# A 2:4-sparse linear layer: one of four rows of the mask product on GpSimd

## The chip, the cores and the metric

The kernel runs on one core of one Trainium2 chip. The metric is the device time of one execution in microseconds (us), the median of several runs. The engines of the core are named as the profile names them: PE (TensorE, matrix products; PEld is its weight loading), DVE (VectorE), ACT (ScalarE), POOL (GpSimd) and SP (SyncE, which here only issues DMAs). Each engine works through its own queue of instructions in order; semaphores order them against each other.

## The reference

```python
B, S, D = 16, 512, 1024          # x: [B,S,D], w: [D,D], b: [D], all bfloat16
def reference(x, w, b):
    N, M = 2, 4
    G = D // M
    wg = w.reshape(G, M, D)
    mag = jnp.abs(wg)
    order = jnp.argsort(mag, 1)
    thr = jnp.take_along_axis(mag, order[:, M - N:M - N + 1, :], 1)
    mask = (lambda x, dt: x.astype(dt))(mag >= thr, w.dtype)
    wp = (wg * mask).reshape(D, D)
    return jnp.einsum("bsd,df->bsf", x, wp) + b
```

Of every four rows of the weight that follow each other, each column keeps the two largest magnitudes and zeroes the others; then comes a dense product of 8192 tokens with the 1024 x 1024 weight, and the bias.

## The kernel before

**Layout of the weight.** The weight is loaded with the four rows of a group side by side in one partition: a tile is [128 partitions, 4, columns], and the index 0 to 3 is the row m of the group. The largest and smallest of pairs, and so the threshold, are then plain elementwise operations along the free dimension.

**Pieces.** The masking is cut into eight pieces (g, first column, last column), g being the half of the input dimension: pieces 0 and 1 are 128 columns each, pieces 2 to 6 are 256, piece 7 is 512. For each, `abs_piece` takes magnitudes (on ACT for pieces 1 and 3 to 7, on DVE for 0 and 2), and `prep_piece` runs seven DVE instructions: hi and lo (largest and smallest of the pairs, L127 and L128), t1 and t2 (L131, L132), the threshold thr (L134), the mask (L136) and the product of the weight with the mask (L137). With 256 columns, mask and product are instructions over 128 x 1024 elements; with 512 columns over 128 x 2048. The mask tile comes from a pool of two buffers, so a mask two pieces later writes into the same memory.

**The front phase.** Seven token tiles (T = 7, 128 tokens each) are multiplied while the weight is still being masked. The order of all engines' work is written out by hand in the string `FRONT` and is kept: W is a dummy matmul, A an abs, P a `prep_piece`, Tgt the transposition of token tile t's half g on PE (four transposes, then a copy to SBUF on ACT, L154), and Mit the four matmuls of piece i for token tile t, one for each row m = 0 to 3 (`mm_piece`, L161). M20 is thus piece 2 for token tile 0, and its fourth matmul, m = 3, reads row 3 of the piece. V copies the finished left half of a bank to SBUF on ACT (L176), S adds the bias to it on DVE (L180), U (`unpack`) starts four DMAs that bring the masked weight into natural order, `wp_nat`, for the main phase (L144, on SP's queue), and B starts a transposing DMA of a batch of token tiles (L197, on SP's queue too).

After the string come the matmuls of piece 7, M70 to M76, with 512 columns, each token tile followed by DVE's addition of the bias out of the bank (`evac_dve`, L184) and a store from ACT's queue (L188).

**The main phase.** Token tiles 7 to 63 are multiplied from `wp_nat` and the transposed batches, 16 matmuls of 512 columns per tile (`mm_nat` at L248 for the first batch and the last tile, L286 for the rest), over eight PSUM banks in turn.

GpSimd builds the identity matrix for the transposes at the start (L101) and has nothing else to do.

Of the kernel before, what the change touches and what calls it, by code (L numbers as in the profile page):

```python
# [10 lines left out]
def kernel(  # L11
# [7 lines left out]
    nc = tc.nc  # L19
# [4 lines left out]
    Alu = mybir.AluOpType  # L24
    Act = mybir.ActivationFunctionType
    K = tc.keep_in_program_order
# [30 lines left out]
    def w_of(i):  # L57
        g, c0, c1 = pieces[i]
        for k, (lg, l0, l1) in loads.items():
            if lg == g and l0 <= c0 and c1 <= l1:  # L60
                return w_ld[k][:, :, c0 - l0:c1 - l0]

    def wp_of(i):
        g, c0, c1 = pieces[i]
        return wp_gh[(g, c0 // FH)][:, :, c0 % FH:c0 % FH + c1 - c0]
# [54 lines left out]
    def prep_piece(i):  # L120
        g, c0, c1 = pieces[i]
        n = c1 - c0
        mag = mags.pop(i)
        magv = mag.rearrange("p (a j) f -> p a j f", j=2)
        hi = tmp.tile([P, 2, FH], bf16, name="hi")[:, :, :n]
        lo = tmp.tile([P, 2, FH], bf16, name="lo")[:, :, :n]
        K(nc.vector.tensor_tensor(hi, magv[:, :, 0, :], magv[:, :, 1, :], op=Alu.max))  # L127
        K(nc.vector.tensor_tensor(lo, magv[:, :, 0, :], magv[:, :, 1, :], op=Alu.min))  # L128
        t1 = tmp.tile([P, FH], bf16, name="t1")[:, :n]
        t2 = tmp.tile([P, FH], bf16, name="t2")[:, :n]  # L130
        K(nc.vector.tensor_tensor(t1, hi[:, 0, :], hi[:, 1, :], op=Alu.min))  # L131
        K(nc.vector.tensor_tensor(t2, lo[:, 0, :], lo[:, 1, :], op=Alu.max))  # L132
        thr = tmp.tile([P, FH], bf16, name="thr")[:, :n]
        K(nc.vector.tensor_tensor(thr, t1, t2, op=Alu.max))  # L134
        mask = tmp.tile([P, 4, FH], bf16, name="mask")[:, :, :n]
        K(nc.vector.tensor_tensor(mask, mag, thr[:, None, :].to_broadcast([P, 4, n]), op=Alu.is_ge))  # L136
        K(nc.vector.tensor_tensor(wp_of(i), w_of(i), mask, op=Alu.mult))  # L137

    wp_nat = [const.tile([P, KT, FH], bf16, name=f"wp_nat{h}") for h in range(2)]

# [74 lines left out]
    for tok in FRONT.split():  # L215
        k, n = tok[0], [int(c) for c in tok[1:]]
        if k == "W":
            warm(1)
        elif k == "A":
            abs_piece(n[0], n[0] in ABS_ON_ACT)  # L220
        elif k == "P":
            prep_piece(n[0])
        elif k == "T":
            g, t = n
            transpose_half(g, t, t if g == 0 else T)
        elif k == "M":
            i, t = n
            mm_piece(i, t, start=i in (0, 5), stop=i in (4, 7))
        elif k == "V":
            evac_act(n[0])  # L230
        elif k == "S":
            add_staged(n[0], 0)
        elif k == "U":
            unpack(*n)
        elif k == "B":
            issue_batch(*batches[n[0]])
# [84 lines left out]
```

## Time and profile before

| | us |
|---|---|
| median of 3 runs (235.44 to 235.93) | 235.66 |
| the profiled execution | 236.1 |
| its span (first to last instruction) | 234.3 |
| PE busy in it | 228.1 |
| DVE busy | 105.7 |
| ACT busy | 18.5 |
| POOL busy | 0.7 |
| product with the mask (L137), 128x512, 128x1024, 128x2048 | 0.426, 0.692, 1.224 |

The span is the time between the first and the last profiled instruction; the execution's time has 1.8 us more around it. A timeline line reads: start in us from the span's start, length, engine, line, operation, output<-inputs, shapes, count; in brackets the engine's idle time before it and what ended it. A line of the groups reads: line, engine, operation, names, shapes, count | busy us, mean ns of one | idle time before and its releaser. The granted TensorE clock was 1.0 for the profiled execution.

### The profile page before, as it was taken

The page shows a single profiled execution, that of the slowest core. Times are in us where ns is not written, and L with a number is a line of the kernel's source. Part 1 is how long each engine was busy: PE and PEld are TensorE (multiplying, and loading weights), DVE is VectorE, ACT ScalarE, POOL GpSimd, SP SyncE. Part 2 cuts the span into 40 slices and gives each one's busy share as a digit, 9 for nine tenths or more (in the row PEclk, how much of TensorE's full clock was granted, in tenths as well). Part 3 has the DMA queues.
Part 4 walks back from the last instruction along what each step waited for, and adds up shares of the span by engine and source line. Part 5 has one row for each costly group of instructions (what it writes and reads, how often), then busy time and mean ns, then how long its engine had stood idle before and what let it go on. Part 6 is the DMA issues. An engine that isn't in the chain of part 4 may idle for free.

```text
span 234.3 us, 2922 instructions
## 1 busy us (share of the span) xinstructions
PE 228.1 (97%) x1197; PEld 114.6 (49%) x1216; DVE 105.7 (45%) x189; ACT 18.5 (8%) x29; POOL 0.7 (0%) x6
## 2 busy tenths in 40 slices
PE   6999999999999999999999999999999999999994
PEld 2889844444444444444444444444444444444453
DVE  3999995342442343344244234334324424433433
ACT  3899000000000000000000000000000000000000
POOL 1000000000000000000000000000000000000000
DMA  6999799999822399216952289221996221122122
GB/s 174 352 243 236 170 210 187 279 209 349 239 93 92 93 213 276 90 48 160 286 151 77 90 215 278 90 92 55 260 304 195 85 90 73 61 90 92 45 90 90
DMA packets 75292, 38.19 MB, mean 163 GB/s; under 512 B 60176, under 2 KB 67088, under 8 KB 75280
## 3 DMA queue, kind: packets, MB, share of 16 engines
q1 hardware_dynamic: 65392, 20.84, 42.6%
q10 hardware_dynamic: 9888, 17.17, 20.3%
q8 instruction: 9, 0.15, 0.3%
q14 instruction: 3, 0.02, 0.0%
HBM read 4.19 MB, written 16.78 MB: 90 GB/s over the span
## 4 chain that ended last, share of the span: by engine, by line
PE 93%; DMA 3%; DVE 2%; issue 1%; SPq 0%
PE bank L286 75%; PE bank L161 9%; PE bank L248 9%; DMA w_B<-in_w_dram 3%; PE bank L152 1%; DVE mask L136 0%; DVE wp L137 0%; SPq L76 0%; SPq L69 0%; DVE mag L116 0%; DVE o_sb L264 0%; DVE hi L127 0%; DVE lo L128 0%; DVE thr L134 0%; DVE t L132 0%
## 5 line engine op out<-in xcount | busy, mean ns | idle before, releaser
L286 PE MATMUL bank<-wp_nat,xTb 128*128 128x512 bf16 x753 | 165.1, 379 | 0.8
L184 DVE TENSOR_TENSOR o_sb<-bank,bias_sb 128x512 bf16<-128x512 f32 x119 | 76.7, 686 | 119.9 <-PE bank L286 108.6
L286 PEld LDWEIGHTS <-xTb 128*128 128x128 bf16 x768 | 75.1, 98 | 90.6
L161 PE MATMUL bank<-wp,xT 128*128 128x256 bf16 (+2 forms) x223 | 26.6, 272 | 0.4
L161 PEld LDWEIGHTS <-xT 128*128 128x128 bf16 x224 | 19.5, 98 | 5.6 <-ACT xT L154 0.7
L248 PE MATMUL bank<-wp_nat,xTs 128*128 128x512 bf16 (+1 forms) x110 | 21.0, 348 | 0.1
L248 PEld LDWEIGHTS <-xTs 128*128 128x128 bf16 x112 | 11.0, 98 | 10.0
L286 PE MATMUL bank<-wp_nat,xTs 128*128 128x512 bf16 x47 | 10.5, 379 | 0.1
L154 ACT COPY xT<-bank 128x512 bf16<-128x512 bf16 x14 | 7.7, 589 | 1.8 <-PE bank L152 1.8
L286 PEld LDWEIGHTS <-xTs 128*128 128x128 bf16 x48 | 4.7, 97 | 5.7
L136 DVE TENSOR_TENSOR mask<-mag,thr 128x1024 bf16<-128x1024 bf16 (+2 forms) x8 | 5.5, 692 | 0.3
L152 PE MATMUL bank<-ident,xh 128*128 128x128 bf16 x56 | 4.8, 219 | 0.7 <-DMA xh<-in_x_dram 0.6
L152 PEld LDWEIGHTS <-xh 128*128 128x128 bf16 x56 | 3.9, 114 | 1.8 <-DMA xh<-in_x_dram 1.5
L105 PE MATMUL bank<-zeros 128*128 128x512 bf16 x8 | 3.5, 625 | 1.2 <-DVE zeros L97 1.2
L180 DVE TENSOR_TENSOR o_sb<-stage,bias_sb 128x512 bf16<-128x512 f32 x7 | 4.3, 682 | 0.0
L176 ACT COPY stage<-bank 128x512 f32<-128x512 f32 x7 | 3.8, 627 | 0.3 <-PE bank L161 0.3
L127 DVE TENSOR_TENSOR hi<-mag 128x512 bf16<-128x512 bf16 (+2 forms) x8 | 3.4, 420 | 0.4 <-ACT mag L114 0.3
L128 DVE TENSOR_TENSOR lo<-mag 128x512 bf16<-128x512 bf16 (+2 forms) x8 | 3.3, 417 | 0.0
L134 DVE TENSOR_TENSOR thr<-t,t 128x256 bf16<-128x256 bf16 (+2 forms) x8 | 2.3, 292 | 0.3
L105 PEld LDWEIGHTS <-zeros 128*128 128x128 bf16 x8 | 1.0, 140 | 2.8 <-issue 1.7
L131 DVE TENSOR_TENSOR t<-hi 128x256 bf16<-128x256 bf16 (+2 forms) x8 | 2.3, 284 | 0.0
L132 DVE TENSOR_TENSOR t<-lo 128x256 bf16<-128x256 bf16 (+2 forms) x8 | 2.3, 284 | 0.0
(21 smaller groups left out, 17.4 us busy)
## 6 DMA issues: line engine op xcount, KB each, us to landing
out_dram<-o_sb ACTq DMA_DIRECT2D x63, 256.0 KB, 3.4
wp_nat<-wp SPq DMA_DIRECT2D x16, 128.0 KB, 2.7
xh<-in_x_dram SPq DMA_DIRECT2D x3, 256.0 KB, 6.1
xh<-in_x_dram ACTq DMA_DIRECT2D x2, 256.0 KB, 5.2
w_C<-in_w_dram SPq DMA_DIRECT2D x1, 512.0 KB, 6.9
w_D<-in_w_dram SPq DMA_DIRECT2D x1, 512.0 KB, 7.9
w_E<-in_w_dram SPq DMA_DIRECT2D x1, 512.0 KB, 8.9
xh<-in_x_dram SPq DMA_DIRECT2D x1, 384.0 KB, 6.8
```

Of the source, the lines that this page charges most:

```text
L105: K(nc.tensor.matmul(bank[7][:], lhsT=zeros[:, :P], rhs=zeros[:], start=True, stop=True))
L127: K(nc.vector.tensor_tensor(hi, magv[:, :, 0, :], magv[:, :, 1, :], op=Alu.max))
L128: K(nc.vector.tensor_tensor(lo, magv[:, :, 0, :], magv[:, :, 1, :], op=Alu.min))
L136: K(nc.vector.tensor_tensor(mask, mag, thr[:, None, :].to_broadcast([P, 4, n]), op=Alu.is_ge))
L152: K(nc.tensor.transpose(dst[:, m, :], xv[:, m, :], ident[:]))
L154: K(nc.scalar.copy(xt[:], dst))
L161: K(nc.tensor.matmul(bank[t][:, o:o + c1 - c0], lhsT=xT[(g, t)][:, m, :], rhs=wp_of(i)[:, m, :], start=start and m == 0, stop=stop and m = ...
L176: K(nc.scalar.copy(st[:], bank[t][:]))
L180: K(nc.vector.tensor_tensor(get_o(t)[:, h * FH:(h + 1) * FH], stage.pop(t)[:], bias_sb[:, h * FH:(h + 1) * FH], op=Alu.add))
L184: K(nc.vector.tensor_tensor(get_o(t)[:, h * FH:(h + 1) * FH], bank[bk][:], bias_sb[:, h * FH:(h + 1) * FH], op=Alu.add))
L248: K(nc.tensor.matmul(bank[bk][:, :c1 - c0], lhsT=xN[t][:, kt, :], rhs=wp_nat[h][:, kt, c0:c1], start=kt == 0, stop=kt == KT - 1))
L286: K(nc.tensor.matmul(bank[bks[h]][:], lhsT=xN[t][:, kt, :], rhs=wp_nat[h][:, kt, :], start=kt == 0, stop=kt == KT - 1))
```

## The change

In `prep_piece`, from the third piece on (i >= 2), the product of the weight with the mask becomes two instructions: GpSimd multiplies row 3, DVE rows 0 to 2. Pieces 0 and 1 keep the one instruction on DVE.

```diff
         K(nc.vector.tensor_tensor(mask, mag, thr[:, None, :].to_broadcast([P, 4, n]), op=Alu.is_ge))
-        K(nc.vector.tensor_tensor(wp_of(i), w_of(i), mask, op=Alu.mult))
+        if i < 2:
+            K(nc.vector.tensor_tensor(wp_of(i), w_of(i), mask, op=Alu.mult))
+        else:
+            K(nc.gpsimd.tensor_tensor(wp_of(i)[:, 3, :], w_of(i)[:, 3, :], mask[:, 3, :], op=Alu.mult))
+            K(nc.vector.tensor_tensor(wp_of(i)[:, :3, :], w_of(i)[:, :3, :], mask[:, :3, :], op=Alu.mult))
```

With it come semaphore waits: each GpSimd product waits for DVE's mask and for the weight's load; the fourth matmul of the first token tile of each piece from 2 to 7 waits for GpSimd; the masks of pieces 4 to 7 wait until GpSimd has read the mask two pieces back; the first DMA of each `unpack` waits for GpSimd beside DVE. The order of instructions on PE, ACT and SP is as before.

## The prediction

> **What bounds the kernel now.** First the page's busy times and its chain that ended last (share of the span by engine and line):
>
> ```profile
> span 234.3 us, 2922 instructions
> PE 228.1 (97%) x1197; PEld 114.6 (49%) x1216; DVE 105.7 (45%) x189; ACT 18.5 (8%) x29; POOL 0.7 (0%) x6
> ...
> PE bank L286 75%; PE bank L161 9%; PE bank L248 9%; DMA w_B<-in_w_dram 3%; PE bank L152 1%; DVE mask L136 0%; DVE wp L137 0%; SPq L76 0%; SPq L69 0%; DVE mag L116 0%; DVE o_sb L264 0%; DVE hi L127 0%; DVE lo L128 0%; DVE thr L134 0%; DVE t L132 0%
> ```
>
> TensorE (PE) is busy for 97% and carries the chain almost alone, so an edit in the mask work can only matter where PE waits for it, and there each microsecond of delay passes to the end. The same chain in order of time (start, length, what) shows the one handover:
>
> ```profile
> 10.82 0.70 DVE wp L137
> 11.52 0.04 issue
> 11.56 1.03 PE bank L161 x8
> ```
>
> Piece 2's product ends at 11.52 and its matmuls M20 start at 11.56. The next views are the timelines of DVE and PE (start, length, what), for the other pieces:
>
> ```profile
> 10.09 0.69 DVE L136 TENSOR_TENSOR mask<-mag,thr 128x1024 bf16<-128x1024 bf16 x1
> 10.82 0.69 DVE L137 TENSOR_TENSOR wp<-w_B,mask 128x1024 bf16<-128x1024 bf16 x1
> 11.83 0.42 DVE L127 TENSOR_TENSOR hi<-mag 128x512 bf16<-128x512 bf16 x1 [0.32 <-ACT mag L114]
> ...
> 14.09 0.69 DVE L137 TENSOR_TENSOR wp<-w_C,mask 128x1024 bf16<-128x1024 bf16 x1
> 14.70 0.42 DVE L127 TENSOR_TENSOR hi<-mag 128x512 bf16<-128x512 bf16 x1
> ...
> 25.70 1.23 DVE L136 TENSOR_TENSOR mask<-mag,thr 128x2048 bf16<-128x2048 bf16 x1
> 26.96 1.22 DVE L137 TENSOR_TENSOR wp<-w_E,mask 128x2048 bf16<-128x2048 bf16 x1
> 28.11 4.29 DVE L180 TENSOR_TENSOR o_sb<-stage,bias_sb 128x512 bf16<-128x512 f32 x7
> ```
>
> ```profile
> 28.24 1.02 PE L161 MATMUL bank<-wp,xT 128*128 128x512 bf16 x3
> ```
>
> From piece 3 on DVE works without a pause (hi starts 0.08 before the product before it ends: 14.70 against 14.78). Piece 7's product ends at 28.18 and M70, the first 512-wide matmul, starts at 28.24; its fourth, m=3, starts at 28.24 + 1.02 − 0.38 (the length of one) = 28.88. PE would have been ready for M70 at 28.16 (the last M66 starts at 28.05, starts of 256-wide ones are 0.11 apart). So piece 7 is just in time with no slack, and M70 is where a late DVE shows. In between PE is ready for M30 at 15.06 (product there at 14.78), M40 at 17.89 (17.63), M50 at 21.17 (20.48), M60 at 25.09 (23.33): slacks of 0.28, 0.26, 0.69 and 1.76.
>
> **The change, part by part.** *Removed from DVE:* one of four rows. Rows of 128x512, 128x1024 and 128x2048 take 0.426, 0.692 and 1.224 us, 0.52 ns an element; so 768 elements cost 0.69 − 256 x 0.52 ns = 0.56 (−0.13) in pieces 2 to 6, and 1536 cost 0.96 (−0.27) in piece 7.
>
> *Added on GpSimd:* five products of 128x256 and one of 128x512. POOL has no product in this trace, so I bound it by its own rows:
>
> ```profile
> masks.py:199 POOL TENSOR_SCALAR_AFFINE_SELECT ident<-ident 128x128 bf16<-128x128 bf16 x1 | 0.3, 292 | 0.1
> masks.py:197 POOL MEMSET ident<- 128x128 bf16 x1 | 0.2, 204 | 0.3 <-POOLq L305 0.3
> ...
> L305 POOL MEMSET const-float32-0.0<- 128x1 f32 x1 | 0.1, 98 | 0.2 <-issue 0.2
> ```
>
> A near-empty instruction is 0.1; the memset adds (204 − 100)/127 = 0.82 ns an element (writing only), the select 1.51 (one input read). Low end, the memset's: 0.31 and 0.52 for 256 and 512 elements. One input: 0.49 and 0.87. High end, the select's slope twice because two inputs are read: 0.87 and 1.65. I take the middle between one input and twice it, nearest to the select: 0.68 and 1.26.
>
> By the Trainium skill, GPSIMD Engine Reference, section 3.1, a fp32 tensor_tensor of 2048 elements takes 4497 ns there; at that rate I estimate 0.56 and 1.12 us, and the sum below would be +2.3 instead of +3.1.
>
> *Two engines on the same data.* Row 3 waits for the same mask as DVE's rows, so both start together after each mask. Nothing before shows POOL and DVE reading SBUF at once (POOL stops at 1.3 us). One end is full overlap, the other that they exclude each other, the one standing still for the whole instruction of the other. ACT's copies and abs run beside DVE's products without stretching them (0.692 beside ACT or not), which speaks for overlap, but it is another engine. I take exclusion: the overlap end can give at most −0.2 (below), and halfway between the ends is already slower than the measurement can miss.
>
> The Trainium skill, SBUF — State Buffer, section "Who interferes with whom", says it outright: a DVE instruction with two SBUF inputs contends with a GpSimd instruction that reads SBUF, and the one issued second is fully blocked. Every DVE instruction from 8.57 to 32.3 is of that kind. By that rule the result is the +3.1, without it −0.2; the trace of before can't say which.
>
> *The sum under exclusion,* DVE first since its own next step starts 0.04 after a mask, POOL next, DVE's following instruction after it:
> - Piece 2: rows 0 to 2 end at 10.82 + 0.56 = 11.38, row 3 at 12.06. Piece 3's hi started at 11.83 (it waits for ACT's abs), now 12.06: +0.23.
> - Each of pieces 3 to 6: −0.13 for the shorter product, +0.08 for the lost overlap of hi, +0.68 for the row: +0.63, four times 2.52. In sum 2.75.
> - Piece 7: rows 0 to 2 end at 28.18 + 2.75 − 0.27 = 30.66, row 3 at 31.92; M70's m=3 starts 0.05 later, at 31.97 instead of 28.88: **+3.1 us**.
>
> The waits of PE ahead of it (row 3 of piece 2: its m=3 starts 12.11 instead of 11.89, +0.2; those of pieces 4 and 5 bring this to about 1.1) are contained in the 3.1, as M70 waits for the DVE stream anyway.
>
> *Added waits and who stands behind them.* The fourth matmul of M20, M30 ... M70 waits for POOL; PE is in order, so the rest of the matmuls and the transposes behind it wait, and behind those ACT's copies of xT, which finish early enough (ACT's last abs ends at 18.9). Masks 4 to 7 wait until POOL has read the mask two pieces back, long done. SP's unpack of each weight block waits for POOL too: U00 is issued at 19.77, 8 us after piece 2; U11 goes some 3.8 late, and so does the first big transposed batch behind it on SP's queue (issued 31.59, landing 13.3 later = 44.9; needed at 51.7, which also moves by 3.1). Hidden: 6 us remain. The seven adds (L180) and the first evacuations go 3.8 late: bank 0 is free at 36.8, and PE wants it again at 36.0 + 3.1. Hidden. No queue changes its order and no DMA is added.
>
> The profiled execution took 236.1 (span 234.3, 1.8 around it): 239.2 by the sum. It lies 0.44 above the median of the runs shown, so the median comes to 235.66 + 3.07 = 238.7.
>
> **The rivals.** *No exclusion* (not slower). GpSimd works beside DVE. Piece 2's rows end at 11.38, M20 starts 0.13 earlier, and row 3 (10.84 + 0.68 = 11.52) is there before m=3 at 11.75. Piece 3 still waits for ACT, then DVE gains 4 x 0.13 + 0.27: piece 7 at 27.4. PE can't use that: it is ready at 28.16 − 0.13 = 28.03, so −0.2: 235.45. For it: POOL is idle, its high price of 0.87 still fits. Against: both engines want the same operands in the same half microsecond.
> *The row is starved.* If DVE keeps its hold as long as its instructions follow without a gap, piece 7's row waits behind the seven adds (L180, 4.2 us on end): 30.66 + 4.2 + 1.26 = 36.1 against 28.88, +7.2: 242.9. For it: hi, lo and the two t run nose to tail. Against: a waiting instruction need not wait for a pause.
> *GpSimd is merely slow,* over 1.4 us for 256 elements, without exclusion: M20's m=3 waits 10.84 + 1.4 − 11.75 = 0.5 or more: about 236.3. Against: twice the select's slope gives 0.87.
>
> **How the numbers follow.** Exclusion 66%: with POOL at its low price the same sum gives +0.6 (piece 3 not pushed, 4 x 0.26, 28.95 + 0.52 + 0.05 − 28.88), at the high price +4.4; if POOL gets in first, all of M70 waits and up to 0.6 is added. Own range 236.2 to 240.7. No exclusion 22%, starved 8%, slow 4%. 0.2% (0.47 us) is about what a measurement tells from no change. Slower: 65 + 8 + 3 = 76%; same 21%; faster 3%, as no case reaches −0.47. The range takes in the rival on the other side and leaves out the starved one: 235.2 to 240.8.
>
> **What would show it.** Right: POOL rows at the product line, DVE's hi after a product later by the length of a POOL instruction or DVE's instructions stretched, M70 near 31. Wrong: DVE's rows and spacing unchanged beside busy POOL rows, and M70 at 28.0. The price is read from POOL's 128x256 rows; starvation from row 3 of piece 7 landing after the adds. From M70 on the spacing of PE must be as before; if not, the hidden transfers weren't.

## The result and the profile after

| | before | after |
|---|---|---|
| median of four runs, us | 235.62 (235.44 to 235.93) | 237.43 (237.37 to 237.53) |
| profiled execution | 236.1 | 237.53 |
| its span | 234.3 | 235.7 |
| piece 2's product starts | 10.82 | 10.56 |
| M70's fourth matmul starts | 28.88 | 30.32 |

The change costs 1.8 us: ratio 1.007, 95% interval 1.0056 to 1.0083. Line numbers after the product are 4 higher in the changed kernel. Its page, busy times and chain:

```profile
PE 229.7 (97%) x1216; PEld 114.8 (49%) x1216; DVE 107.6 (46%) x189; ACT 18.5 (8%) x29; POOL 7.8 (3%) x12
...
PE 87%; DVE 4%; issue 3%; DMA 2%; ACT 1%; POOL 1%; POOLq 1%; SPq 0%; DVEq 0%
```

DVE gave six rows away and is recorded as busy for 1.9 us more, not less; and POOL has come into the chain. Where, the timelines of the changed kernel show (start, length, what). DVE, with the product of piece 3, what follows it, and piece 7:

```profile
13.78 0.56 DVE L141 TENSOR_TENSOR wp<-w_C,mask 128x768 bf16<-128x768 bf16 x1
14.25 0.89 DVE L127 TENSOR_TENSOR hi<-mag 128x512 bf16<-128x512 bf16 x1
15.07 0.41 DVE L128 TENSOR_TENSOR lo<-mag 128x512 bf16<-128x512 bf16 x1
...
15.92 0.29 DVE L134 TENSOR_TENSOR thr<-t,t 128x256 bf16<-128x256 bf16 x1
16.31 0.69 DVE L136 TENSOR_TENSOR mask<-mag,thr 128x1024 bf16<-128x1024 bf16 x1
17.04 0.56 DVE L141 TENSOR_TENSOR wp<-w_C,mask 128x768 bf16<-128x768 bf16 x1
...
28.30 0.96 DVE L141 TENSOR_TENSOR wp<-w_E,mask 128x1536 bf16<-128x1536 bf16 x1
29.17 5.25 DVE L184 TENSOR_TENSOR o_sb<-stage,bias_sb 128x512 bf16<-128x512 f32 x7
```

POOL at the same places:

```profile
13.82 1.04 POOL L140 TENSOR_TENSOR wp<-w_C,mask 128x256 bf16<-128x256 bf16 x1 [2.17 <-DVE mask L136]
17.09 1.04 POOL L140 TENSOR_TENSOR wp<-w_C,mask 128x256 bf16<-128x256 bf16 x1 [2.22 <-DVE mask L136]
...
28.34 1.92 POOL L140 TENSOR_TENSOR wp<-w_E,mask 128x512 bf16<-128x512 bf16 x1 [3.69 <-DVE mask L136]
```

The rows of piece 4 in the kernel before:

```profile
15.88 0.29 DVE L134 TENSOR_TENSOR thr<-t,t 128x256 bf16<-128x256 bf16 x1
16.21 0.69 DVE L136 TENSOR_TENSOR mask<-mag,thr 128x1024 bf16<-128x1024 bf16 x1
16.94 0.69 DVE L137 TENSOR_TENSOR wp<-w_C,mask 128x1024 bf16<-128x1024 bf16 x1
```

PE at M70, in the changed kernel:

```profile
29.31 0.81 PE L165 MATMUL bank<-wp,xT 128*128 128x512 bf16 x3 [1.03 <-DVE wp L141]
30.32 5.55 PE L165 MATMUL bank<-wp,xT 128*128 128x512 bf16 x25 [0.20 <-POOL wp L140]
```

DVE's product is as short as forecast (0.56 and 0.96) although POOL has started beside it. The hi behind it is recorded with 0.89 instead of 0.42: it starts 0.08 before the product's end, as before, and then stands still for 0.47 (0.89 − 0.42). POOL's row ends at 13.82 + 1.04 = 14.86, in the middle of that hi. From product to product (13.78 to 17.04) it is now 3.26 us; before it was 2.85 (14.09 to 16.94). Of the 0.41 more, −0.13 is the shorter product, +0.47 the stretched hi, and +0.07 lies ahead of the mask, which starts 0.10 after thr's end (15.92 + 0.29 = 16.21, mask 16.31) where it was 0.03 (16.17 and 16.21 by the rounded figures of the rows above). Piece 7's row 3 lands at 30.26, 1.00 after DVE's rows (29.26), and the seven adds behind them take 5.25 instead of 4.29, all of it in the first one (1.64 instead of 0.68).

PE is idle for 1.03 us until DVE's rows of piece 7 are there and for 0.20 more until GpSimd's is: M70's fourth matmul starts 0.58 after the third (30.32 against 29.74), where 0.22 is the spacing. From M70's fourth matmul to the end of the chain's last matmul it is 202.5 us in both executions (28.88 to 231.34, 30.32 to 232.77): nothing behind it was stretched. Measured from piece 2's product, the fourth matmul of M70 comes 19.76 us later against 18.06 before: +1.70. The spans differ by 1.4 and not by 1.70 because piece 2's product started 0.26 earlier in this execution; in the one before, by its chain, piece 2 still waited for its weight's load. Executions of the kernel before differ by more than that among themselves (235.44 to 235.93).

### The profile page after: what moved, and what is told of

It is laid out like the page before. It is cut to its first block, busy times and chain, and to the rows that moved or that the text cites. A ratio compares the mean times of both kernels' runs of the same rounds, so it can differ in the third digit from the quotient of the medians.

```text
span 235.7 us, 2955 instructions
## 1 busy us (share of the span) xinstructions
PE 229.7 (97%) x1216; PEld 114.8 (49%) x1216; DVE 107.6 (46%) x189; ACT 18.5 (8%) x29; POOL 7.8 (3%) x12
## 4 chain that ended last, share of the span: by engine, by line
PE 87%; DVE 4%; issue 3%; DMA 2%; ACT 1%; POOL 1%; POOLq 1%; SPq 0%; DVEq 0%
PE bank L290 75%; PE bank L252 9%; PE bank L165 3%; DMA xh<-in_x_dram 2%; ACT xT L158 1%; DVE mask L136 1%; POOL wp L140 1%; DVE hi L127 1%; POOLq L320 1%; PE bank L156 1%; DVE wp L141 0%; DVE lo L128 0%; ACT mag L114 0%; DVE thr L134 0%; DVE t L132 0%
## 5 line engine op out<-in xcount | busy, mean ns | idle before, releaser
L127 DVE TENSOR_TENSOR hi<-mag 128x512 bf16<-128x512 bf16 (+2 forms) x8 | 5.3, 658 | 0.5 <-ACT mag L114 0.4
L184 DVE TENSOR_TENSOR o_sb<-stage,bias_sb 128x512 bf16<-128x512 f32 x7 | 5.2, 815 | 0.0
L268 DVE TENSOR_TENSOR o_sb<-bank,bias_sb 128x256 bf16<-128x256 f32 x4 | 1.7, 422 | 1.2 <-PE bank L252 1.2
```

The source lines that it names most:

```text
L184: K(nc.vector.tensor_tensor(get_o(t)[:, h * FH:(h + 1) * FH], stage.pop(t)[:], bias_sb[:, h * FH:(h + 1) * FH], op=Alu.add))
```

## The experiments

The theories at stake: A, the two engines exclude each other (DVE's product first, then GpSimd's row, then DVE's next), and the slip, with the time ahead of each mask as the price of its second wait, adds up over the pieces; B, the loss is the last row alone; C, the time ahead of the mask (0.06 in the expectations) is an after-effect of GpSimd's reading and not of the wait; D, GpSimd simply is slow and runs beside DVE; E, what costs is PE's new waits. Two more come with later runs: F, a collision has a fixed price; G, any access of GpSimd to SBUF blocks DVE.

**Pieces 2 to 6 alone.** Piece 7 stays whole on DVE.

```diff
-        if i < 2:
+        if i < 2 or i == 7:
```

> GpSimd takes row 3 of pieces 2 to 6, piece 7 stays whole on VectorE. Theory A (slip): each of pieces 3 to 7 starts 0.40 us later than the one before it had it (row taken off -0.13, GpSimd's hold +0.47, a second wait at the mask +0.06), so piece 7's product ends some 1.6 us later and M70 with it: about 1.6 over before, hardly less than the whole change (+1.8). Theory B (last row): the loss is mostly the row of piece 7 itself, which lands 1.0 us behind VectorE's rows; then this run is within 0.8 of before.

Measured: ratio 1.0056 (1.0034 to 1.0079, which is 0.8 to 1.9 us), 237.29 us beside 235.76 for the kernel before. The last product of DVE and the first matmul in its timelines:

```profile
27.94 1.22 DVE L138 TENSOR_TENSOR wp<-w_E,mask 128x2048 bf16<-128x2048 bf16 x1
```

```profile
29.22 4.04 PE L165 MATMUL bank<-wp,xT 128*128 128x512 bf16 x17 [1.29 <-DVE wp L138]
```

The product ends at 29.16, 18.93 after piece 2's product started (10.23); before it was 17.36. That is +1.57, as theory A had it, of the change's +1.70: most of the loss is there without GpSimd having any part in piece 7.

**Piece 7 alone.**

```diff
-        if i < 2:
+        if i < 7:
```

> Only piece 7 gives its row to GpSimd. Theory A: VectorE's rows end 0.27 earlier, at 27.9; GpSimd's row about 1.0 later, at 28.9, and M70's fourth matmul wanted it at 28.9 anyway: within 0.2 of before. Theory B: M70 waits the row's whole length behind VectorE's: +0.8 or more.

Measured: ratio 0.9998 (0.9985 to 1.0010), no difference. DVE and POOL at piece 7:

```profile
26.83 0.96 DVE L141 TENSOR_TENSOR wp<-w_E,mask 128x1536 bf16<-128x1536 bf16 x1
```

```profile
26.88 1.92 POOL L140 TENSOR_TENSOR wp<-w_E,mask 128x512 bf16<-128x512 bf16 x1 [25.58 <-DVE mask L136]
```

DVE's rows end at 27.79 (26.83 + 0.96), GpSimd's at 28.80 (26.88 + 1.92), 18.06 after piece 2's product started (10.74). That is when M70's fourth matmul started in the kernel before (18.06), so it wants its row at about that time anyway. Theory B falls.

**The mask in place.** The whole change, but mask is written over the magnitudes of its own piece, so no mask waits for GpSimd.

```diff
-        mask = tmp.tile([P, 4, FH], bf16, name="mask")[:, :, :n]
+        mask = mag
```

> The whole change, but each mask is written over its piece's own magnitudes, so no mask waits for GpSimd to free a buffer; the contention stays. Theory A: the 0.06 us that each of the masks of pieces 4 to 7 starts later is the second wait's; it goes, and the time falls by 0.25 against the change (from +1.8 to about +1.55). Theory C: the 0.06 is an after-effect of GpSimd's use of the buffers' port; then the masks start as late as in the change and the time is the change's.

Measured: ratio 1.0061 (1.0039 to 1.0082), 237.28. The time alone can't be told from the change's 1.0070. The trace can tell. The mask of piece 4, which is called mag here, starts 0.03 after thr's end (15.95 + 0.29 = 16.24):

```profile
15.95 0.29 DVE L134 TENSOR_TENSOR thr<-t,t 128x256 bf16<-128x256 bf16 x1
16.27 0.69 DVE L136 TENSOR_TENSOR mag<-mag,thr 128x1024 bf16<-128x1024 bf16 x1
```

Products follow each other by 3.20 (13.80, 17.00, 20.20, 23.39) instead of 3.26, and M70's fourth matmul starts at 30.07 instead of 30.32, with piece 2's product at 10.58 against 10.56. That is 0.27 less (19.49 after piece 2's product instead of 19.76), though GpSimd reads as much as in the change. So the 0.07 is the mask's second wait, four times, and theory C falls.

**A row into scratch.** DVE multiplies all four rows, and GpSimd does row 3 once more into a tile that nobody reads.

```diff
+        if i >= 2:
+            scr = const.tile([P, n], bf16, name=f"scr_{i}")
+            K(nc.gpsimd.tensor_tensor(scr[:], w_of(i)[:, 3, :], mask[:, 3, :], op=Alu.mult))
+        K(nc.vector.tensor_tensor(wp_of(i), w_of(i), mask, op=Alu.mult))
```

> VectorE multiplies all four rows as before, and GpSimd multiplies row 3 as well, into a scratch tile nobody reads. No matmul and no DMA waits for GpSimd. Theory A (exclusion, GpSimd second): GpSimd's recorded length contains its wait for VectorE's product, which is 0.13 longer, so its 256-element row is recorded with 1.17 instead of 1.04; the next hi is still stretched by 0.47; the slip is 0.53 a piece, 2.1 at piece 7, and the time 2.1 over before, more than the change. Theory D (GpSimd simply takes 4 ns an element beside VectorE and hi's stretch has another cause): the length stays 1.04. Theory E (what costs is PE waiting for GpSimd): the time is that of before.

Measured: ratio 1.0102 (1.0077 to 1.0128), 238.41, 1.8 to 3.0 us over before. Its four runs (238.1 to 238.53) all lie above those of the change (237.37 to 237.53), which were measured at another time, beside a before of 235.62 instead of 235.76. POOL, and DVE's product and hi beside it:

```profile
14.23 1.17 POOL L139 TENSOR_TENSOR scr<-w_C,mask 128x256 bf16<-128x256 bf16 x1 [2.15 <-DVE mask L136]
```

```profile
14.19 0.69 DVE L140 TENSOR_TENSOR wp<-w_C,mask 128x1024 bf16<-128x1024 bf16 x1
14.79 0.89 DVE L127 TENSOR_TENSOR hi<-mag 128x512 bf16<-128x512 bf16 x1
```

The same GpSimd instruction is recorded with 1.17 instead of 1.04 because DVE's product ahead of it is 0.13 longer: its length contains its wait. Theory D wanted 1.04. No matmul waits for GpSimd here and the time is the longest so far, so theory E falls too: what costs is DVE's delay, 0.54 a piece (products at 14.19, 17.58, 20.98, 24.37), the 0.47 of hi and the 0.07 of the mask.

**GpSimd products in the main phase.** The kernel before, with 24 products added whose results nobody reads; in even token tiles beside DVE's second evacuation, in odd ones while DVE is idle.

```diff
             for h in range(2):
                 evac_dve(t, h, bks[h])
+            if t >= 20 and t < 44:
+                n = 256 if t % 4 < 2 else 512
+                o = out_tiles[t][:, (t % 2) * FH:(t % 2) * FH + n]
+                K(nc.gpsimd.tensor_tensor(wp_gh[(0, 0)][:, t % 4, :n], o, w_ld["E"][:, 0, :n], op=Alu.mult))
             store(t)
```

> The kernel before, with 24 GpSimd products more in the main phase (token tiles 20 to 43), whose results nobody reads. In even tiles the product reads the left half of the output tile and so runs beside VectorE's second evacuation, which reads one operand in SBUF and one in PSUM; in odd tiles it reads the right half and runs when VectorE has nothing to do. 256 elements in half of them, 512 in the others. Theory A (exclusion by two-operand SBUF reads; 1.04 and 1.92 us contain the wait for VectorE's product): alone 0.5 to 0.6 for 256 and 1.0 to 1.1 for 512, the same beside an evacuation, and evacuations stay at 0.69. Theory D (GpSimd takes 4 ns an element): 1.04 and 1.92, alone too. Time as before in either.

One run: 236.15 us, beside 235.58 to 236.6 for the kernel before on that chip. POOL's timeline for four of them (even, odd, even, odd), and DVE's evacuations as a group (line, names, shapes, count | busy us, mean ns), first in that stretch, then those of the whole kernel before, from its page:

```profile
82.93 0.67 POOL L293 TENSOR_TENSOR wp<-o_sb,w_E 128x256 bf16<-128x256 bf16 x1 [81.63 <-DVE o_sb L184]
86.98 0.67 POOL L293 TENSOR_TENSOR wp<-o_sb,w_E 128x256 bf16<-128x256 bf16 x1 [3.38 <-DVE o_sb L184]
89.83 1.15 POOL L293 TENSOR_TENSOR wp<-o_sb,w_E 128x512 bf16<-128x512 bf16 x1 [2.19 <-DVE o_sb L184]
93.88 1.16 POOL L293 TENSOR_TENSOR wp<-o_sb,w_E 128x512 bf16<-128x512 bf16 x1 [2.90 <-DVE o_sb L184]
```

```profile
L184 DVE TENSOR_TENSOR o_sb<-bank,bias_sb 128x512 bf16<-128x512 f32 x42 | 27.1, 686 | 45.5 <-PE bank L286 26.0 <-issue 15.2 <-POOL wp L293 4.3
```

```profile
L184 DVE TENSOR_TENSOR o_sb<-bank,bias_sb 128x512 bf16<-128x512 f32 x119 | 76.7, 686 | 119.9 <-PE bank L286 108.6
```

Undisturbed, the product takes 0.67 and 1.15: (1.15 − 0.67)/256 = 1.9 ns an element and 0.19 fixed. Beside an evacuation, whose one input is in PSUM and the other in SBUF, it takes the same, and the evacuation keeps its 0.686 (the 12 that overlap a product have 0.68 each). The expected figures lay about 0.1 us too low; what they were to tell apart is clear: theory D's 1.04 and 1.92 aren't the price.

**Nothing, one or two operands read.** The kernel before; behind DVE's whole product GpSimd clears row 3 of the used mask (pieces 3 and 6), copies a row (piece 4) or multiplies (piece 5).

```diff
         K(nc.vector.tensor_tensor(wp_of(i), w_of(i), mask, op=Alu.mult))
+        if i in (3, 6):
+            K(nc.gpsimd.memset(mask[:, 3, :], 0.0))
+        if i in (4, 5):
+            scr = const.tile([P, n], bf16, name=f"scr_{i}")
+            if i == 4:
+                K(nc.gpsimd.tensor_copy(scr[:], wp_of(i)[:, 3, :]))
+            else:
+                K(nc.gpsimd.tensor_tensor(scr[:], w_of(i)[:, 3, :], wp_of(i)[:, 3, :], op=Alu.mult))
```

> The kernel before, VectorE's products whole; behind the product of pieces 3 and 6 GpSimd sets row 3 of the used mask to zero (reads nothing), behind piece 4 it copies row 3 of the product into scratch (reads one operand), behind piece 5 it multiplies (reads two). Each starts when VectorE is in the hi of the next piece, so what it blocks is lo or t1. Theory A: no stretch at the memsets; lo or the next one is stretched by about 0.5 at the product, and by half of that (0.2 to 0.3) at the copy, as one operand instead of two goes through. Theory G (any access of GpSimd to SBUF blocks VectorE): the memsets stretch it as well.

One run, made for its trace. POOL, and DVE when POOL runs: hi and lo of piece 4, lo of pieces 5 and 6:

```profile
14.48 0.31 POOL L139 MEMSET mask<- 128x256 bf16 x1 [13.18 <-DVE wp L137]
17.34 0.53 POOL L143 COPY scr<-wp 128x256 bf16<-128x256 bf16 x1 [2.55 <-DVE wp L137]
20.48 0.78 POOL L145 TENSOR_TENSOR scr<-w_D,wp 128x256 bf16<-128x256 bf16 x1 [2.62 <-DVE wp L137]
```

```profile
14.34 0.42 DVE L127 TENSOR_TENSOR hi<-mag 128x512 bf16<-128x512 bf16 x1
14.68 0.42 DVE L128 TENSOR_TENSOR lo<-mag 128x512 bf16<-128x512 bf16 x1
...
17.53 0.62 DVE L128 TENSOR_TENSOR lo<-mag 128x512 bf16<-128x512 bf16 x1
...
20.65 0.89 DVE L128 TENSOR_TENSOR lo<-mag 128x512 bf16<-128x512 bf16 x1
```

The memset (14.48 to 14.79) runs mostly beside hi and a little beside lo; both keep their 0.42, and its 0.31 is what the forecast's two POOL rows give for a memset of 256 elements. Beside a copy lo is 0.20 longer, beside a product 0.47. Writing doesn't block, reading does, and two operands (one product) for more than twice as long as one (one copy). So it is the reading of SBUF that the two engines can't do at once, and theory G falls. This run also bears out the mask's second wait: piece 5's mask, whose memory the memset of piece 3 wrote, is the only one that starts 0.10 after thr's end; the others start 0.03 after it.

**Two rows.** GpSimd takes rows 2 and 3.

```diff
-            K(nc.gpsimd.tensor_tensor(wp_of(i)[:, 3, :], w_of(i)[:, 3, :], mask[:, 3, :], op=Alu.mult))
-            K(nc.vector.tensor_tensor(wp_of(i)[:, :3, :], w_of(i)[:, :3, :], mask[:, :3, :], op=Alu.mult))
+            K(nc.gpsimd.tensor_tensor(wp_of(i)[:, 2:, :], w_of(i)[:, 2:, :], mask[:, 2:, :], op=Alu.mult))
+            K(nc.vector.tensor_tensor(wp_of(i)[:, :2, :], w_of(i)[:, :2, :], mask[:, :2, :], op=Alu.mult))
```

> GpSimd takes rows 2 and 3 instead of row 3 alone. Theory A with the measured sizes (1.9 ns an element of hold against 0.52 that VectorE saves, and 0.06 at the mask): a slip of -0.27 + 0.97 + 0.06 = 0.76 a piece, 0.3 at piece 3 and 4 x 0.76 behind it; rows 0 and 1 of piece 7 end at 31.0, GpSimd's rows at 33.0 where M70's third matmul wanted them at 28.7: 4.0 to 4.8 over before. Theory F (a collision costs a fixed 0.47): a slip of 0.26 a piece, 1 to 2 over before.

Measured: ratio 1.0223 (1.0182 to 1.0263), a median of 241.01 beside 235.68: 5.3 over before, more than the 4.0 to 4.8 expected. Of the four runs (240.12 to 241.75) the two longest were granted a TensorE clock of 0.993, the others 1.0. The profiled execution took 240.48, 4.4 over the profiled one of before (236.1), as expected. DVE's hi after the product, and PE's M70:

```profile
18.34 1.37 DVE L127 TENSOR_TENSOR hi<-mag 128x512 bf16<-128x512 bf16 x1
```

```profile
33.02 5.77 PE L165 MATMUL bank<-wp,xT 128*128 128x512 bf16 x26 [1.38 <-POOL wp L140]
```

hi stands still for 0.95 (1.37 − 0.42), the hold of 512 elements; the pieces follow each other by 3.62 (2.85 + 0.77), and M70's third matmul starts at 33.02, all as theory A had worked it out from one row (0.76 a piece, 33.0). The cost grows with the elements; theory F's fixed price falls.

No version that beats both kernels came out of this. In the front phase every element handed over takes 1.9 ns of the reading that DVE needs too, in place of DVE's 0.52, so a smaller share should only lose less; piece 7 alone, where nothing was lost, gained nothing either. Other shares were not tried.

## Why the prediction was right in its direction and too large

*The bound.* Right: PE had no slack at M70, and what arrived late there arrived late at the end, with the same 202.5 us behind it.

*Exclusion, with DVE first.* Right, and it was the forecast's main choice. The row in scratch, the run with memset, copy and product, and the two rows show it. The Trainium skill, SBUF — State Buffer, section "Who interferes with whom", has the rule in the form that the runs support: two-operand DVE instructions collide with a GpSimd instruction that reads SBUF (lo +0.47), not with one that only writes (hi and lo unchanged), and an evacuation with one operand in SBUF doesn't collide (0.686). The Trainium skill, SBUF — State Buffer, section "SBUF: two separate sides", says that the one that starts first holds the shared ports for its whole instruction; here DVE stood still for 0.47 of the 0.67 that the product takes alone, so the measured hold is shorter.

*The price of GpSimd's product.* 0.68 and 1.26 forecast, 0.67 and 1.15 measured undisturbed. That 0.68 fits is partly luck: it was the middle of two guesses and holds 0.10 fixed and 2.3 ns an element, where 0.19 and 1.9 were measured. The forecast also meant to read the price from POOL's 128x256 rows; these show 1.04, because they contain the wait. The failed step is the next one: the sum let DVE stand still for the instruction's whole length. The hold is 0.47 for 256 elements and about 0.96 for 512 (hi +0.95 with two rows; the adds behind piece 7, 5.25 − 4.29), 1.9 ns an element with nothing fixed. The traces show where the other 0.2 goes. In every collision GpSimd's row ends 0.52 to 0.53 after the end of the DVE instruction ahead of it (14.86 against 14.34), and 1.00 to 1.02 with 512 elements, whatever the length of that instruction; so about 0.14 of the 0.67 or 1.15 passes beside DVE, before the hold, and the last 0.05 or so after it. What GpSimd does in these parts no run shows.

*The sum by its terms, from piece 2's product.* Piece 3: +0.23 forecast, −0.05 measured (14.09 − 10.82 = 3.27 against 13.78 − 10.56 = 3.22), since the shorter hold was over at 11.51 (11.12 − 0.08 + 0.47) and hi, which waits for ACT's abs, started at 11.53 anyway. The four steps behind it: 0.63 each forecast, 0.41 measured: the hold −0.21, the lost overlap of hi −0.08 (hi still starts 0.08 early; the 0.47 is all there is), and the mask's second wait +0.07, which the forecast had named but costed at nothing. Piece 7's row: 1.26 behind DVE's rows forecast, 1.00 measured. The terms of the forecast as written add up to 3.09 (it goes on with 3.07). Together 3.09 − 0.28 − 0.88 − 0.26 = 1.67, against 1.70 measured.

*Hidden work.* Right: the transposed batch was issued at 32.83 instead of 31.59, the evacuations began at 34.35 instead of 32.32, and nothing waited for them.

*The rivals.* No exclusion is refuted by the 1.17 of the row in scratch. A starved row is refuted by piece 7: its row landed 1.00 behind DVE's rows, before the seven adds were through, though DVE's instructions follow without a gap. Slow GpSimd is refuted by 0.67. The order within a collision, DVE first, held in all six pieces.

## What to carry to other kernels

Moving part of a chain of two-operand VectorE instructions to an idle GpSimd wasn't parallel work here: both read SBUF, one at a time, and each bf16 element of the product cost GpSimd 1.9 ns of that where VectorE needs 0.52. Look for the loss in the instruction after the one that was shortened: it is recorded as longer, not as waiting, and GpSimd's own recorded length contains its wait. In these runs GpSimd held VectorE up neither where VectorE read one operand from PSUM, nor where it was idle, nor with work that only writes (a memset).

## What the runs showed of the hardware that was not expected

A second semaphore wait on a DVE instruction, for something long done, costs 0.07 us: the mask starts 0.10 after thr's end with it and 0.03 without, in every run. A GpSimd copy of 256 elements holds DVE up for 0.20 (seen once), a product for 0.47, more than two copies.
